# Attention in front of two mixtures of experts: another sequence for float64 weights, and two operations on other engines

## The chip, the cores and the metric

The kernel runs on one core of a Trainium2 chip. The metric is the device time of one execution, in microseconds. Five engines work in parallel, each through its own queue in the order in which the program issues its instructions: TensorE (PE in the profile, its weight loads PEld), VectorE (DVE), ScalarE (ACT), GpSimd (POOL) and SyncE (SP), which here issues all DMA transfers. An instruction starts when those ahead of it on its engine are through and when what it reads or overwrites is ready; the program inserts waits on semaphores for that.

## The reference

Three stages follow one another: causal block attention over 32 heads, a dense layer pair with `h * cos(h)`, and an eight-expert layer pair whose gates are balanced by eight rounds of row and column normalisation.

```python
scores = scale * np.matmul(q, k.transpose(0, 1, 3, 2))        # 32 heads, 576 x 64
scores = np.where(mask, scores, -1000000000.0)                # blocks of 64
scores = scores - np.max(scores, axis=-1, keepdims=True)
attn = np.exp(scores)
attn = attn / (np.sum(attn, axis=-1, keepdims=True) + 1e-09)
x = np.matmul(attn, v)                                        # to 2304 x 512
...
h = x @ w_in                                                  # w_in, w_out: float64
x = (h * np.cos(h)) @ w_out
...
for e in range(E):                                            # 8 experts
    out += P[:, e:e + 1] * (np.maximum(x @ w1[e], 0.0) @ w2[e])
```

`moe_w_in` and `moe_w_out` arrive as float64. The core has to make float32 of them itself, from the two 32-bit words of each number.

## The kernel before

All matmuls that matter run on pairs of a high and a low part of each float32 operand. The order of the work is written out by hand: each engine gets its instructions in the order in which the Python code issues them, and no scheduler moves them. What the text calls head i is one turn of the loop over the 32 heads in `attention()`.

In head i, TensorE takes the second half of the row maxima of head i + 1, the scores of head i and their product with v. Names that the text uses, with their lines:

- `px` (L265, `peak`): scores for the row maxima of the next head, in two halves u = 0 and u = 1 that share one PSUM tile. VectorE reduces each half into `nm` (L279), two reductions for u = 0 and three for u = 1. TensorE can write the second half only when the reductions of the first are done.
- `ep`, `eq`, `er`, `ec` (L303, L309, L315, L320): the exponentials on ScalarE. The start of `ep` is taken as the start of a head.
- `hi_q` (L228, L229), `hi_k` (L232), `lo` (L237 kb, L239 qb), `move` (L245, L246): the high parts of q and k for head i + 2 on ScalarE and VectorE, the low parts on GpSimd, copies between partitions by DMA.
- `turn`, `maxima` (L283, L287): the maxima of head i + 1 are transposed on TensorE and put in place by VectorE.
- `evac` (L347): ScalarE copies a head's output out of PSUM. `sums`, `fetch`, `invert` (L359), `give`, `spread` (L368): the row sums of a pair of heads are sent through DRAM, inverted on VectorE and spread over 64 partitions into `RB`.
- `scale` (L376): the division, as a product of 64 x 576 on GpSimd, into the tile `XF`. `x_hi` (L379, ScalarE) and `x_lo` (L383, GpSimd) split `XF` into the operands of the next stage.

The division runs behind the heads by pairs. In an even head i it multiplies head i - 4, in an odd head i head i - 5; at the end of the odd head follow `x_hi` and `x_lo` for both. `XF` is one buffer (a slice of a `tt` tile):

```python
RB, XF = tt[1][:, 0:S], tt[2][:, 0:S]
...
for i in range(NH):
    work = i % 6 != 5
    if i >= 4:
        scale(i - 4 - i % 2, i % 2)
    ...
    if work:
        some(2 if i else 1)
    ...
    if odd and i >= 5:
        x_hi(i - 5)
        x_lo(i - 5)
```

The conversion of the float64 weights (class `Conv`) is a generator whose steps are strewn over the heads by `some(n)`: 32 half tiles of 128 x 512, five steps each, five steps in a head, and none in every sixth head (`work`). A half tile is loaded two halves ahead (L87, 512 KB). `exponent` (L92, VectorE) takes the exponent out of the high word, `limits` (L98, L99, ScalarE) clips it and turns it into the bits of a power of two, `mantissa` (L111, L115, VectorE) builds the upper 21 and 16 further bits as a float, and `product` puts the sign onto the power (L122, VectorE) and multiplies (L124, GpSimd). The halves that are left over are converted in the first blocks of the next stage, in which GpSimd also makes the low parts of that stage's weights (L68).

Where the last heads' divisions end, the next stage's weight tiles (`jh`, L65) take over the memory that the division reads. The last two products of the pairs stand in that stage, in a table of left-over work (`leftover`).

Of the kernel before, what the change touches and what calls it, by code (L numbers as in the profile page):

```python
# [10 lines left out]
F32 = mybir.dt.float32  # L11
F32R = mybir.dt.float32r
BF16 = mybir.dt.bfloat16
I32 = mybir.dt.int32
U16 = mybir.dt.uint16
AF = mybir.ActivationFunctionType
ALU = mybir.AluOpType
# [4 lines left out]
N, DM = B * S, H * D  # L22
# [12 lines left out]
EPS = 1e-9  # L35
MASK = -1.0e30
TWO_PI = 2.0 * np.pi


@with_exitstack  # L40
def attention_moe_kernel(ctx: ExitStack, tc: tile.TileContext, qk, v, w_a, gate, w_b, out):
    nc = tc.nc
    top = ctx.enter_context(tc.tile_pool(name="top", bufs=1))
# [7 lines left out]
    nc.vector.memset(half_pi, float(np.pi / 2))  # L51
    eps = top.tile([128, 2], F32, name="eps")
    nc.vector.memset(eps, 0.0)
    e_max = top.tile([128, 1], F32, name="e_max")
    nc.vector.memset(e_max, 1171.0)
    e_all = top.tile([128, 1], F32, name="e_all")
    nc.vector.memset(e_all, 255.0 * 2.0 ** 23)


    xh = top.tile([128, NC, N], F32R, name="xh")  # L60
# [12 lines left out]
    NHALF = 2 * F1  # L73

    class Conv:
# [10 lines left out]
            src = w_a[k // 2].bitcast(I32).rearrange("p (n w) -> p n w", w=2)  # L86
            nc.sync.dma_start(out=self.w64[k], in_=src[:, (k % 2) * DM:(k % 2 + 1) * DM, :])  # L87

        def exponent(self, k):

            sc = self.sc[k] = self.scratch(1, k, [128, DM])
            nc.vector.tensor_scalar(out=sc, in0=self.w64[k][:, :, 1], scalar1=1, scalar2=21,  # L92
                                    op0=ALU.logical_shift_left, op1=ALU.logical_shift_right)

        def limits(self, k):

            sc = self.sc[k]
            nc.scalar.activation(sc, sc, AF.Relu, bias=e_max, scale=-1.0)  # L98
            nc.scalar.activation(sc, sc, AF.Relu, bias=e_all, scale=-2.0 ** 23)  # L99

        def part(self, k):
            f, o = k // 2, (k % 2) * DM
            return raw[f][:, o:o + DM]

        def mantissa(self, k):

            if k % 2 == 0:
                raw[k // 2] = wp.tile([128, 2 * DM], F32, tag="w", name="raw")
            m, w64 = self.part(k), self.w64[k]
            m21 = m.bitcast(I32)  # L110
            nc.vector.tensor_scalar(out=m21, in0=w64[:, :, 1], scalar1=0xFFFFF, scalar2=0x100000,  # L111
                                    op0=ALU.bitwise_and, op1=ALU.bitwise_or)
            yield
            mid = w64.rearrange("p n w -> p (n w)").bitcast(U16).rearrange("p (n q) -> p n q", q=4)[:, :, 1]
            nc.vector.scalar_tensor_tensor(out=m, in0=mid, scalar=2.0 ** -16, in1=m21,  # L115
                                           op0=ALU.mult, op1=ALU.add)
            yield

        def product(self, k):

            sc, m = self.sc.pop(k), self.part(k)
            nc.vector.scalar_tensor_tensor(out=sc, in0=self.w64.pop(k)[:, :, 1], scalar=-2 ** 31, in1=sc,  # L122
                                           op0=ALU.bitwise_and, op1=ALU.bitwise_or)
            nc.gpsimd.tensor_tensor(out=m, in0=m, in1=sc.bitcast(F32), op=ALU.mult)  # L124

        def run(self):

            self.load(0)
            self.load(1)
            for k in range(NHALF):  # L130
                if k:
                    self.product(k - 1)
                    if k + 1 < NHALF:
                        self.load(k + 1)
                yield
                self.exponent(k)
                yield
                self.limits(k)
                yield
                yield from self.mantissa(k)  # L140
            self.product(NHALF - 1)
            yield


# [3 lines left out]
    def attention():  # L148
        with tc.tile_pool(name="at1", bufs=1) as p1, tc.tile_pool(name="at2", bufs=2) as p2, \
# [9 lines left out]
            KA = [p1.tile([128, S], F32R, name=f"ka{j}") for j in range(2)]  # L159
# [18 lines left out]
            st, EP, EQ, ER, EC, SUMS, INV, ps_t, ps_o = ({} for _ in range(9))  # L178
# [50 lines left out]
                nc.scalar.activation(HI[64:128, :], st[i][64:128, :], AF.Copy)  # L229

            def hi_k(i):
                nc.vector.tensor_copy(out=KA[i % 2][0:64, :], in_=st[i][0:64, :])  # L232

            def lo(i):

# [137 lines left out]

            def scale(e, h):
                r = slice(64 * h, 64 * h + 64)
                nc.gpsimd.tensor_tensor(out=XF[r, :], in0=RAW[e // 2 % 2][h][r, :], in1=RB[r, :], op=ALU.mult)  # L376

            def x_hi(e):
                nc.scalar.activation(xh[:, place(e)[0], place(e)[1]], XF, AF.Copy)  # L379
# [79 lines left out]
            e = NH - 2  # L459
# [7 lines left out]
    with tc.manual_schedule():  # L467
# [174 lines left out]
        def open_group(g):  # L642

            X[g] = psh.tile([128, TB], F32, tag="h", name="hx")
            product(g, X[g], "A11", "B11", True)
            Y[g] = psh.tile([128, TB], F32, tag="h", name="hy")
            product(g, Y[g], "S1", "T1", True)


        def moe1():  # L650
            nonlocal th, tl
            with tc.tile_pool(name="m1", bufs=2) as p:
# [14 lines left out]
                def h_unit(n):  # L667
# [184 lines left out]
        for g in range(NG + 1):  # L852
            now, w = g < NG, Weights(g + 1) if g + 1 < NG else None
# [100 lines left out]
```

## Time and profile before

| | |
|---|---|
| median of 3 runs | 2243.87 us (2243.08 to 2244.49) |
| profiled execution, first to last instruction (span) | 2242.3 us |
| TensorE busy | 2158.4 us (96%) |
| VectorE busy | 1571.1 us (70%) |
| GpSimd busy | 1115.1 us (50%) |
| ScalarE busy | 1020.5 us (46%) |
| mean granted TensorE clock | 0.992 of full speed |

The profiled execution's own time is its span, 2242.3 us from its first to its last instruction; the work around it is in the runs' times alone. The busy shares are means over stages that have different limits: attention lasts from 0 to about 265 us, the dense layers to about 710, the experts take the rest. Times in the rows are us from the span's start unless marked ns. An arrow in square brackets names what ended an engine's idle time before an instruction, with that time.

### The profile page before, as it was taken

What the parts mean: (1) busy time and instruction counts of PE and PEld (TensorE: products, weight loads), DVE (VectorE), ACT (ScalarE), POOL (GpSimd) and SP (SyncE); (2) the same over time, 40 slices, a digit from 0 to 9 for tenths busy, and PEclk for the clock granted to TensorE, in tenths of its full rate; (3) what the DMA queues carried; (4) which work ended last, traced back from release to release, by engine and by line L of the source; (5) the groups of instructions that cost most, each with busy time, mean ns of one, the idle gap of its engine ahead of it and who ended that gap; (6) DMA issues with size and microseconds to landing.
All of it is one profiled execution on the core that took longest, in us unless ns stands there. A gap on an engine that the chain in (4) does not pass through costs nothing.

```text
span 2242.3 us, 29534 instructions
## 1 busy us (share of the span) xinstructions
PE 2158.4 (96%) x10869; PEld 1910.0 (85%) x10869; DVE 1571.1 (70%) x2477; ACT 1020.5 (46%) x1882; POOL 1115.1 (50%) x928
## 2 busy tenths in 40 slices
PE   7888789999998999999999999999999999999999
PEld 4555589998997888888888888888988888888988
DVE  8888776676666876666676666666676666666665
ACT  5666655555555333433344333433444434333432
POOL 5888785665554334343554434343554434344341
PEclk9999999999999999999999999999999999999999
DMA  5666410000001112121221312121221312121220
GB/s 154 167 165 175 123 34 1 1 1 1 1 19 53 61 57 75 57 76 57 76 64 50 118 61 76 57 76 58 74 69 50 118 57 76 57 76 62 71 73 31
DMA packets 74160, 152.83 MB, mean 68 GB/s; under 512 B 32896, under 2 KB 32896, under 8 KB 74016
## 3 DMA queue, kind: packets, MB, share of 16 engines
q1 hardware_dynamic: 74016, 150.95, 21.7%
q8 instruction: 85, 1.39, 0.3%
q14 instruction: 59, 0.48, 0.1%
HBM read 136.91 MB, written 4.87 MB: 63 GB/s over the span
## 4 chain that ended last, share of the span: by engine, by line
PE 64%; DVE 3%; ACT 1%; issue 0%; ACTq 0%; DVEq 0%
PE acc L474 11%; PE acc L476 11%; PE acc L475 11%; PE hx L476 6%; PE hx L474 6%; PE hx L475 6%; PE hy L474 3%; PE hy L476 3%; PE hy L475 3%; PE hz L474 1%; PE hz L475 1%; PE hz L476 1%; DVE wal L576 0%; ACT hh L810 0%; DVE hl L811 0%; DVE tl L68 0%
## 5 line engine op out<-in xcount | busy, mean ns | idle before, releaser
L585 POOL TENSOR_TENSOR wv<-stg,wv 128x512 fp32r<-128x512 f32 x190 | 335.7, 1788 | 852.7 <-ACT wv L584 852.7
L474 PE MATMUL acc<-wv,hh 128*128 128x512 f32 x1152 | 456.3, 396 | 0.0
L476 PE MATMUL acc<-wv,hl 128*128 128x512 f32 x1152 | 455.6, 395 | 0.0
L475 PE MATMUL acc<-wv,hh 128*128 128x512 f32 x1152 | 454.5, 395 | 0.0
L839 DVE SCALAR_TENSOR_TENSOR oa<-acc,P,oa 128x512 f32<-128x512 f32 x540 | 379.0, 740 | 5.2 <-PE acc L476 4.3
L810 ACT ACTIVATE hh<-c 128x384 fp32r<-128x384 f32 x288 | 151.3, 525 | 409.6 <-DVE c L896 166.0
L68 POOL TENSOR_TENSOR jl<-raw,jh 128x512 fp32r<-128x512 f32 x190 | 253.5, 1344 | 168.5 <-ACT jh L65 166.5
L811 DVE SCALAR_TENSOR_TENSOR hl<-c,hh 128x384 fp32r<-128x384 f32 x288 | 163.9, 569 | 176.4 <-ACT hh L810 176.4
L476 PEld LDWEIGHTS acc<-wv,hl 128*128 128x128 f32 x1152 | 216.0, 187 | 53.7
L475 PEld LDWEIGHTS acc<-wv,hh 128*128 128x128 f32 x1152 | 215.9, 187 | 44.0
L474 PEld LDWEIGHTS acc<-wv,hh 128*128 128x128 f32 x1152 | 216.1, 188 | 43.0
L890 DVE TENSOR_TENSOR c<-hz,c 128x384 f32<-128x384 f32 x96 | 53.4, 556 | 192.0 <-PE hz L476 192.0
L880 ACT ACTIVATE c<-hx 128x384 f32<-128x384 f32 x96 | 47.4, 494 | 282.7 <-PE hx L476 282.7
L576 DVE TENSOR_TENSOR wal<-s,wah 128x1024 fp32r<-128x1024 f32 x96 | 172.2, 1793 | 0.0
L65 ACT ACTIVATE jh<-raw 128x512 fp32r<-128x512 f32 x192 | 119.3, 622 | 99.4 <-PE acc L475 86.7
L476 PE MATMUL h<-xh,jl 128*128 128x384 f32 x384 | 132.2, 344 | 10.3 <-POOL jl L68 10.2
L687 DVE TENSOR_TENSOR hl<-g,hh 128x384 fp32r<-128x384 f32 x96 | 100.7, 1048 | 56.8 <-ACT hh L685 56.8
L474 PE MATMUL h<-xh,jh 128*128 128x384 f32 x384 | 131.6, 343 | 9.1 <-ACT jh L65 8.9
L474 PE MATMUL acc<-hh,jh 128*128 128x384 f32 x384 | 129.4, 337 | 2.2 <-DVE xl L705 1.3
L474 PE MATMUL hy<-xh,wah 128*128 128x384 f32 x384 | 129.2, 337 | 1.3 <-DVE c L896 1.3
L475 PE MATMUL h<-xl,jh 128*128 128x384 f32 x384 | 130.2, 339 | 0.0
L476 PE MATMUL hy<-xh,wal 128*128 128x384 f32 x384 | 129.1, 336 | 0.7 <-DVE wal L576 0.7
(214 smaller groups left out, 5158.4 us busy)
## 6 DMA issues: line engine op xcount, KB each, us to landing
stg<-in_w_b_dram SPq DMA_DIRECT2D x192, 512.0 KB
cw<-in_w_a_dram SPq DMA_DIRECT2D x32, 512.0 KB
st<-in_qk_dram SPq DMA_DIRECT2D x64, 144.0 KB
v<-in_v_dram SPq DMA_DIRECT2D x31, 160.0 KB
tt<-inv SPq DMA_DIRECT2D x32, 144.0 KB
out_dram<-oa SPq DMA_DIRECT2D x18, 256.0 KB
kb<-ka SPq DMA_DIRECT2D x31, 144.0 KB
qb<-qa SPq DMA_DIRECT2D x31, 144.0 KB
```

Source lines behind the costliest of these rows:

```text
L65: nc.scalar.activation(hi, src, AF.Copy)
L68: eng_lo.tensor_tensor(out=lo, in0=src, in1=hi.bitcast(F32), op=ALU.subtract)
L474: nc.tensor.matmul(ps, lh, rh, start=first, stop=False, skip_group_check=go_on)
L475: nc.tensor.matmul(ps, lh, rl, start=False, stop=False, skip_group_check=go_on)
L476: nc.tensor.matmul(ps, ll, rh, start=False, stop=last, skip_group_check=go_on)
L576: eng.tensor_tensor(out=self.al, in0=self.s, in1=self.ah.bitcast(F32), op=ALU.subtract)
L585: eng.tensor_tensor(out=t[:, DM:2 * DM], in0=src, in1=t[:, 0:DM].bitcast(F32), op=ALU.subtract)
L687: nc.vector.tensor_tensor(out=G[n][1], in0=g, in1=G[n][0].bitcast(F32), op=ALU.subtract)
L810: nc.scalar.activation(hh, src, AF.Relu)
L811: nc.vector.scalar_tensor_tensor(out=hl, in0=src, scalar=0.0, in1=hh.bitcast(F32), op0=ALU.max, op1=ALU.subtract)
L839: nc.vector.scalar_tensor_tensor(out=o, in0=acc, scalar=p, in1=o, op0=ALU.mult, op1=ALU.add)
L890: nc.vector.tensor_tensor(out=c[0], in0=z, in1=c[0], op=ALU.add)
```

## The change

The change replaces the conversion's sequence, and moves two operations.

- The conversion: `magnitude` takes the absolute value of the high word, read as float32, on ScalarE. `rounding` turns the upper 16 bits of the low word into a small integer, on ScalarE, and writes it over the low word. `clamp` and `shift` bring the magnitude into the range and place of a float32, on VectorE. `bits` puts the sign on, on VectorE, and `add` adds the small integer as int32, on GpSimd. Five steps a half tile are kept.
- `hi_k` moves from VectorE to ScalarE.
- `scale`, the division's product, moves from GpSimd to VectorE.

```diff
-        def exponent(self, k):
-            nc.vector.tensor_scalar(out=sc, in0=self.w64[k][:, :, 1], scalar1=1, scalar2=21,
-                                    op0=ALU.logical_shift_left, op1=ALU.logical_shift_right)
-        def limits(self, k):
-            nc.scalar.activation(sc, sc, AF.Relu, bias=e_max, scale=-1.0)
-            nc.scalar.activation(sc, sc, AF.Relu, bias=e_all, scale=-2.0 ** 23)
-        def mantissa(self, k):
-            nc.vector.tensor_scalar(out=m21, in0=w64[:, :, 1], scalar1=0xFFFFF, scalar2=0x100000,
-                                    op0=ALU.bitwise_and, op1=ALU.bitwise_or)
-            yield
-            nc.vector.scalar_tensor_tensor(out=m, in0=mid, scalar=2.0 ** -16, in1=m21,
-                                           op0=ALU.mult, op1=ALU.add)
-        def product(self, k):
-            nc.vector.scalar_tensor_tensor(out=sc, in0=self.w64.pop(k)[:, :, 1], scalar=-2 ** 31, in1=sc,
-                                           op0=ALU.bitwise_and, op1=ALU.bitwise_or)
-            nc.gpsimd.tensor_tensor(out=m, in0=m, in1=sc.bitcast(F32), op=ALU.mult)
+        def magnitude(self, k):
+            nc.scalar.activation(self.sc[k].bitcast(F32), self.high(k).bitcast(F32), AF.Abs)
+        def rounding(self, k):
+            nc.scalar.activation(w64[:, :, 0], mid, AF.Copy, scale=2.0 ** -13)
+        def clamp(self, k):
+            nc.vector.tensor_scalar(out=sc, in0=sc, scalar1=LEAST, scalar2=MOST, op0=ALU.max, op1=ALU.min)
+        def shift(self, k):
+            nc.vector.tensor_scalar(out=sc, in0=sc, scalar1=3, scalar2=0x3FFFFFF8,
+                                    op0=ALU.logical_shift_left, op1=ALU.bitwise_and)
+        def bits(self, k):
+            nc.vector.scalar_tensor_tensor(out=self.part(k).bitcast(I32), in0=self.high(k), scalar=-2 ** 30,
+                                           in1=self.sc.pop(k), op0=ALU.bitwise_and, op1=ALU.bitwise_or)
+        def add(self, k):
+            nc.gpsimd.tensor_tensor(out=m, in0=m, in1=self.w64.pop(k)[:, :, 0], op=ALU.add)
...
         def run(self):
...
                 if k:
-                    self.product(k - 1)
+                    self.add(k - 1)
                     if k + 1 < NHALF:
                         self.load(k + 1)
                 yield
-                self.exponent(k)
+                self.magnitude(k)
                 yield
-                self.limits(k)
+                self.rounding(k)
+                self.clamp(k)
                 yield
-                yield from self.mantissa(k)
-            self.product(NHALF - 1)
+                self.shift(k)
+                yield
+                self.bits(k)
+                yield
+            self.add(NHALF - 1)
...
             def hi_k(i):
-                nc.vector.tensor_copy(out=KA[i % 2][0:64, :], in_=st[i][0:64, :])
+                nc.scalar.activation(KA[i % 2][0:64, :], st[i][0:64, :], AF.Copy)
...
             def scale(e, h):
-                nc.gpsimd.tensor_tensor(out=XF[r, :], in0=RAW[e // 2 % 2][h][r, :], in1=RB[r, :], op=ALU.mult)
+                nc.vector.tensor_tensor(out=XF[r, :], in0=RAW[e // 2 % 2][h][r, :], in1=RB[r, :], op=ALU.mult)
```

The diff is cut to its core: lines that only name views of the same tiles and two constants that fall away are left out. In the changed kernel the lines of `attention()` stand four further down.

How the queues read before and after is shown at three places. In these rows "waits" lists the semaphores that an instruction waits for, by the engine that raises them (Pool is GpSimd, DMAHW are transfers). Where nothing is listed, the order of the queue or an earlier wait covers it.

VectorE, from the end of an odd head to the next even head (heads 7 and 8), before:

```order
L287 TENSOR_TENSOR qa_100<-pt,diag 5x640 [waits PE_49]
L111 TENSOR_SCALAR raw<-cw 128x512
L115 SCALAR_TENSOR_TENSOR raw<-cw,raw 128x512 [waits DVE_49]
L279 TENSOR_REDUCE nm_110<-px 128x1 [waits PE_49]
L279 TENSOR_REDUCE nm_110<-px 128x1
L122 SCALAR_TENSOR_TENSOR tla<-cw,tla 128x512 [waits Activation_49]
L92 TENSOR_SCALAR tla<-cw 128x512 [waits DMAHW5_49,Pool_49]
```

VectorE at the same place in the changed kernel (L291 is L287 of before, L107 clamp, L111 shift, L118 bits, L380 the division's product into `XF`, a `tt` tile, L283 the reductions):

```order
L107 TENSOR_SCALAR tla<-tla 128x512 [waits Activation_49]
L291 TENSOR_TENSOR qa_96<-pt,diag 5x640 [waits PE_49]
L111 TENSOR_SCALAR tla<-tla 128x512 [waits DVE_49]
L118 SCALAR_TENSOR_TENSOR raw<-cw,tla 128x512 [waits DMAHW4_49,DVE_49]
L380 TENSOR_TENSOR tt<-tla,tt 64x576 [waits DMAHW6_49,Pool_49]
L283 TENSOR_REDUCE nm_106<-px 128x1 [waits PE_49]
```

The conversion's steps between the reductions are gone, and the product with a wait for GpSimd stands ahead of them.

GpSimd, from an odd head into the next even head, before (L124 the conversion's product, L237 kb, L239 qb, L383 x_lo, L376 the division's product):

```order
L376 TENSOR_TENSOR tt<-tt 64x576 [waits DMAHW5_49]
L124 TENSOR_TENSOR raw<-raw,tla 128x512 [waits DVE_49,Pool_49]
L237 TENSOR_TENSOR kb_107<-st,ka_103 64x576 [waits DMAHW6_49,DVE_49,PE_49]
L239 TENSOR_TENSOR qb_105<-st,hi 64x576 [waits DMAHW7_49,Activation_49,Pool_49]
L383 TENSOR_TENSOR xl<-tt,xh 128x576 [waits Activation_49,Pool_49]
L376 TENSOR_TENSOR tt<-tla,tt 64x576 [waits DMAHW6_49,Pool_49]
L124 TENSOR_TENSOR raw<-raw,tla 128x512 [waits DVE_49]
```

GpSimd at the same place in the changed kernel (L124 is now the add, L241 kb, L243 qb, L387 x_lo):

```order
L124 TENSOR_TENSOR raw<-raw,cw 128x512 [waits DVE_49,DMAHW3_49,Activation_49,Pool_49]
L241 TENSOR_TENSOR kb_103<-st,ka_99 64x576 [waits DMAHW6_49,PE_49,Activation_49]
L243 TENSOR_TENSOR qb_101<-st,hi 64x576 [waits DMAHW7_49,Pool_49]
L387 TENSOR_TENSOR xl<-tt,xh 128x576 [waits Activation_49,Pool_49]
L124 TENSOR_TENSOR raw<-raw,cw 128x512 [waits DMAHW4_49,DVE_49]
```

Both products of the division are gone from the queue. kb now waits for ScalarE (Activation), where k's high part is made, and x_lo is followed by the add.

ScalarE in an odd head of the changed kernel, from the last exponential on (L96 magnitude, L232 and L233 q's high part, L236 k's, L102 rounding, L383 x_hi):

```order
L324 ACTIVATE ec<-sc 64x64 [waits PE_49,Activation_49]
L96 ACTIVATE tla<-cw 128x512 [waits DMAHW4_49]
L232 ACTIVATE qa_97<-st 64x576 [waits DMAHW7_49,DMAHW1_49]
L233 ACTIVATE hi<-st 64x576 [waits Activation_49,Pool_49]
L236 ACTIVATE ka_99<-st 64x576 [waits DMAHW6_49,DMAHW0_49]
L102 ACTIVATE cw<-cw 128x512
L383 ACTIVATE xh<-tt 128x576 [waits DVE_49]
```

Before, two passes of `limits` stood behind q's high part; now one pass of the conversion stands ahead of it, and k's high part is between.

## Rows read from the trace of the kernel before

**Rows 1.** Busy time by stretch: us, engines' busy us, clock, DMA share, GB/s

```profile
150.00:200.00 50.00, 40.84 (x193) 27.84 (x191) 44.08 (x69) 34.74 (x61) 41.80 (x28) 0.97 0.60 163
...
400.00:500.00 100.00, 98.82 (x566) 96.72 (x565) 70.28 (x108) 54.87 (x101) 60.87 (x46) 1.00 0.00 1
```

**Rows 2.** First exponential of each head, whole run, then 60 to 255 us

```profile
L303 ACT ACTIVATE ep<-sp x32: 583/599/604, 17.1 to 259.9; 128x512 f32<-128x512 f32 x32
...
L303 ACT ACTIVATE ep<-sp x25: 597/599/602, 62.0 to 253.3; 128x512 f32<-128x512 f32 x25
```

**Rows 3.** Who waited for whom, TensorE, 60 to 255 us: total, times, longest

```profile
PE px L265 <- DVE nm L279: 24.9, 20, 1.7
```

**Rows 4.** Conversion on VectorE, 60 to 255 us: ns minimum/median/maximum

```profile
L122 DVE SCALAR_TENSOR_TENSOR tla<-cw,tla x21: 679/682/1075, 62.8 to 254.1; 128x512 int32<-128x512 int32 x21
...
L92 DVE TENSOR_SCALAR tla<-cw x20: 416/420/1723, 63.7 to 239.8; 128x512 int32<-128x512 int32 x20
...
L111 DVE TENSOR_SCALAR raw<-cw x20: 426/685/939, 67.8 to 243.8; 128x512 int32<-128x512 int32 x20
...
L115 DVE SCALAR_TENSOR_TENSOR raw<-cw,raw x20: 1795/1802/1811, 68.7 to 244.8; 128x512 f32<-128x512 uint16 x20
```

**Rows 5.** Timeline of head 18: start, us, engine, line; GpSimd and VectorE together

```profile
159.05 1.72 POOL L376 TENSOR_TENSOR tt<-tla,tt 64x576 f32<-64x576 f32 x1
...
159.44 1.71 DVE L92 TENSOR_SCALAR tla<-cw 128x512 int32<-128x512 int32 x1
```

**Rows 6.** Timeline of head 17, ScalarE

```profile
148.29 0.74 ACT L347 ACTIVATE tla<-o,eps 65x576 f32<-65x576 f32 x1 [0.96 <-PE o L341]
...
149.46 0.60 ACT L303 ACTIVATE ep<-sp 128x512 f32<-128x512 f32 x1 [0.43 <-PE sp L296]
...
151.38 0.68 ACT L228 ACTIVATE qa<-st 64x576 fp32r<-64x576 f32 x1
```

**Rows 7.** Timeline of head 17, hand-over from VectorE to GpSimd

```profile
154.00 0.44 DVE L232 CAST ka<-st 64x576 fp32r<-64x576 f32 x1
...
154.58 1.40 POOL L237 TENSOR_TENSOR kb<-st,ka 64x576 fp32r<-64x576 f32 x1 [2.40 <-issue]
...
157.54 1.43 POOL L383 TENSOR_TENSOR xl<-tt,xh 128x576 fp32r<-128x576 f32 x1
```

**Rows 8.** Prices of single forms: groups (count, busy us, mean ns), timeline of head 15

```profile
L68 DVE TENSOR_TENSOR jl<-raw,jh 128x512 fp32r<-128x512 f32 x2 | 1.3, 690 | 5.8 <-ACT jh L65 5.8
...
136.99 1.32 POOL L124 TENSOR_TENSOR raw<-raw,tla 128x512 f32<-128x512 f32 x1 [0.96 <-DVE tla L122]
...
L98 ACT ACTIVATE tla<-tla,e_max 128x512 int32<-128x512 int32 x20 | 14.4, 722 | 6.6 <-DVE tla L92 6.4
```

**Rows 9.** A weight load of head 14 (timeline, SP), and a later stretch

```profile
129.38 0.34 SPq L87 DMA_DIRECT2D cw<-in_w_a_dram  x1
...
135.00:135.50 0.50, 0.13 (x2) 0.00 (x0) 0.50 (x1) 0.50 (x2) 0.50 (x1) 1.00 0.00 0
```

**Rows 10.** Timeline of head 14, VectorE and ScalarE: reductions to the next head

```profile
127.46 1.29 DVE L279 TENSOR_REDUCE nm<-px 128x1 f32<-128x448 f32 x2
...
133.73 0.60 ACT L303 ACTIVATE ep<-sp 128x512 f32<-128x512 f32 x1 [0.41 <-PE sp L296]
```

**Rows 11.** Busy time by stretch in head 13 (columns as in rows 1)

```profile
118.50:120.00 1.50, 0.00 (x0) 0.00 (x0) 1.47 (x4) 1.45 (x4) 1.18 (x1) 1.00 0.08 9
...
120.50:124.00 3.50, 3.50 (x8) 1.72 (x7) 1.77 (x5) 2.02 (x3) 2.84 (x3) 0.51 0.85 251
```

**Rows 12.** Timeline behind the attention stage: waits in square brackets

```profile
267.19 1.39 POOL L376 TENSOR_TENSOR tt<-raw,tt 64x576 f32<-64x576 f32 x1
...
268.62 1.67 ACT L65 ACTIVATE jh<-raw 128x512 fp32r<-128x512 f32 x3 [3.46 <-POOL tt L376]
...
303.44 0.68 ACT L379 ACTIVATE xh<-tt 128x576 fp32r<-128x576 f32 x1 [4.78 <-POOL tt L376]
...
305.20 0.69 PE L474 MATMUL h<-xh,jh 128*128 128x384 f32 x1 [2.87 <-ACT jh L65]
```

More of the change, by code (lines that the diff above doesn't have):

```diff
@@ L37 @@
 TWO_PI = 2.0 * np.pi
+LEAST, MOST = (float(np.array([b], np.uint32).view(np.float32)[0]) for b in (0x38100000, 0x47EFFFFF))
 @with_exitstack
@@ L53, in attention_moe_kernel @@
     nc.vector.memset(eps, 0.0)
[L54 to L57, printed above, removed]
     xh = top.tile([128, NC, N], F32R, name="xh")
@@ L87, in load, with high @@
             nc.sync.dma_start(out=self.w64[k], in_=src[:, (k % 2) * DM:(k % 2 + 1) * DM, :])
-        def exponent(self, k):
-            sc = self.sc[k] = self.scratch(1, k, [128, DM])
-            nc.vector.tensor_scalar(out=sc, in0=self.w64[k][:, :, 1], scalar1=1, scalar2=21,
-                                    op0=ALU.logical_shift_left, op1=ALU.logical_shift_right)
-        def limits(self, k):
-            sc = self.sc[k]
-            nc.scalar.activation(sc, sc, AF.Relu, bias=e_max, scale=-1.0)
-            nc.scalar.activation(sc, sc, AF.Relu, bias=e_all, scale=-2.0 ** 23)
+        def high(self, k):
+            return self.w64[k][:, :, 1]
         def part(self, k):
@@ L103, in part @@
             return raw[f][:, o:o + DM]
-        def mantissa(self, k):
+        def magnitude(self, k):
+            self.sc[k] = self.scratch(1, k, [128, DM])
+            nc.scalar.activation(self.sc[k].bitcast(F32), self.high(k).bitcast(F32), AF.Abs)
+        def rounding(self, k):
+            w64 = self.w64[k]
+            mid = w64.rearrange("p n w -> p (n w)").bitcast(U16).rearrange("p (n q) -> p n q", q=4)[:, :, 1]
+            nc.scalar.activation(w64[:, :, 0], mid, AF.Copy, scale=2.0 ** -13)
+        def clamp(self, k):
+            sc = self.sc[k].bitcast(F32)
+            nc.vector.tensor_scalar(out=sc, in0=sc, scalar1=LEAST, scalar2=MOST, op0=ALU.max, op1=ALU.min)
+        def shift(self, k):
+            sc = self.sc[k]
+            nc.vector.tensor_scalar(out=sc, in0=sc, scalar1=3, scalar2=0x3FFFFFF8,
+                                    op0=ALU.logical_shift_left, op1=ALU.bitwise_and)
+        def bits(self, k):
             if k % 2 == 0:
                 raw[k // 2] = wp.tile([128, 2 * DM], F32, tag="w", name="raw")
-            m, w64 = self.part(k), self.w64[k]
-            m21 = m.bitcast(I32)
-            nc.vector.tensor_scalar(out=m21, in0=w64[:, :, 1], scalar1=0xFFFFF, scalar2=0x100000,
-                                    op0=ALU.bitwise_and, op1=ALU.bitwise_or)
-            yield
-            mid = w64.rearrange("p n w -> p (n w)").bitcast(U16).rearrange("p (n q) -> p n q", q=4)[:, :, 1]
-            nc.vector.scalar_tensor_tensor(out=m, in0=mid, scalar=2.0 ** -16, in1=m21,
-                                           op0=ALU.mult, op1=ALU.add)
-            yield
-        def product(self, k):
-            sc, m = self.sc.pop(k), self.part(k)
-            nc.vector.scalar_tensor_tensor(out=sc, in0=self.w64.pop(k)[:, :, 1], scalar=-2 ** 31, in1=sc,
-                                           op0=ALU.bitwise_and, op1=ALU.bitwise_or)
-            nc.gpsimd.tensor_tensor(out=m, in0=m, in1=sc.bitcast(F32), op=ALU.mult)
+            nc.vector.scalar_tensor_tensor(out=self.part(k).bitcast(I32), in0=self.high(k), scalar=-2 ** 30,
+                                           in1=self.sc.pop(k), op0=ALU.bitwise_and, op1=ALU.bitwise_or)
+        def add(self, k):
+            m = self.part(k).bitcast(I32)
+            nc.gpsimd.tensor_tensor(out=m, in0=m, in1=self.w64.pop(k)[:, :, 0], op=ALU.add)
         def run(self):
```

## Prediction

> **What bounds the kernel now.** I began with the busy table by stage. In the MoE stages TensorE is busy 98.8 of 100 us, in attention 40.8 of 50, where VectorE has 44.1 and GpSimd 41.8 [rows 1]. The MoE stages are the multiplier's own; whatever the change does, it does in attention and just behind it. So next I read the length of a head, from one start of `ep` (the first exponential, L303) to the next: heads 0 to 31 start at 17.1 to 259.9 us, heads 6 to 30 at 62.0 to 253.3 [rows 2]. That is 191.3 / 24 = 7.97 us a head, **47.8 us for six heads** (the pattern repeats after six, since every sixth head carries no weight conversion), and (62.0 - 17.1) / 6 = 7.48 us in the first six heads, which have no division yet. The waits then say who holds TensorE: the second half of the score maxima (`px`) waits for VectorE's reductions of the first half (`nm`), 24.9 us in 20 waits, 1.25 us each [rows 3]. VectorE is late because the conversion stands ahead of those reductions in its queue: the sum L115 takes 1.80 us every time, the others 0.42 to 1.72 [rows 4].
>
> Why so long: L92 began 0.39 us into a GpSimd multiply of 1.72 us and took 1.71 us, where its fastest is 0.42 [rows 4, 5]. It ended 0.38 us behind that multiply. So a VectorE operation of this kind stands still until GpSimd's running one ends, and the saved work must be priced with that.
>
> **Part by part.** VectorE loses, for each half tile, L92, L111 and L115, and once a head the high part of k (0.44 us [rows 7]). It gains clamp and shift, priced as L92 and L111, their nearest forms: 0.42 us each if nothing blocks, up to 1.72 if GpSimd does [rows 4]. The `bits` operation is of L122's form, 0.68 to 1.08 [rows 4]. The division's product comes to VectorE: 0.69 us for 512 columns [rows 8], so 0.78 for 576 (estimate by columns). By the medians VectorE is relieved of 0.42 + 0.69 + 1.80 + 0.44 - 0.42 - 0.42 - 0.78 = 1.7 us in a head with conversion. ScalarE swaps two passes of 0.72 for two of the same size (bounds 0.60, an exponential of that width, to 0.72 [rows 6, 8]) and gains k's high part, 0.68 by its sister L228 [rows 6]. GpSimd loses the product and swaps a float product for an integer add, taken at 1.32 as that product ran unhindered [rows 8]. No row shows an integer add there. Half or twice that are the bounds: it counts once in six heads below, so 0.66 x 4.33 = 2.9 us less or 1.32 x 4.33 = 5.7 more.
>
> On SP no transfer moves, but the load of the next half tile now waits for GpSimd's add where it waited for VectorE's sign step, and q, k and the copies stand behind it. In the chain below the add of an even head ends about 11.6 us after the odd head's `ep`; the half is first read at 17.5 + 1.9 = 19.4. A load issued at 129.38 had landed by 135.0, when no DMA engine moved anything [rows 9]: 5.6 us at most against 7.8 of room, so nothing. If that room went, ScalarE would stand at `magnitude` with q's and k's high parts behind it.
>
> **The new wait** is what I base the number on. `XF` is one buffer. GpSimd's x_lo reads it late in every odd head, and the product of the next even head overwrites it. Both were GpSimd's, in order. Now the product is VectorE's, it must wait for x_lo, and both reductions of `px` queue behind it. Followed from `ep` of an odd head:
> - four exponentials until the q copy starts: 151.38 - 149.46 = 1.92 [rows 6];
> - magnitude 0.72, two q copies and k's, 3 x 0.68: 2.76, so 4.68;
> - hand-over to GpSimd 154.58 - 154.44 = 0.14, then kb, qb and x_lo, 157.54 + 1.43 - 154.58 = 4.39 [rows 7]: 9.21;
> - hand-over 0.14, product 0.78, reductions 1.29 [rows 10]: 11.42;
> - from there TensorE's own queue to the next `ep`: 133.73 - 128.75 = 4.98 in an even head [rows 10]: **16.40 us for two heads**.
>
> Where the odd head has no conversion, the magnitude falls out: 15.68. Six heads take at least 2 x 16.40 + 15.68 = 48.5 us, 0.7 more than now, although VectorE has less to do.
>
> To this come the waits of VectorE and GpSimd for one another. In a head with conversion, shift and bits (0.42 + 0.68) are queued ahead of the product while kb, qb and x_lo run, and get in between them: 17.50. Without conversion the add of the half before is ready when x_lo ends and goes first, 1.32: 17.00. Six heads: 52.0, **4.2 more than now**. If the add goes ahead of the product in the other pairs too, 18.82 and 54.6: 6.8 more. Bounds 0.7 and 6.8; I take 4.2, as the rows of L92 and L115 show such waits as the rule. Heads 6 to 31 are 4.33 times six: +18.2 (3.0 to 29.5).
>
> The Trainium skill (page SBUF — State Buffer, section Who interferes with whom) says that a VectorE operation with two SBUF inputs, or in a two-port mode, and a GpSimd operation reading SBUF exclude each other for whole instructions: "the other fully blocks". It speaks against this change, since the product on VectorE still contends with GpSimd. The trace agrees (1.71 us for 0.42 of work). With that rule the sum is 52.0 for six heads, without it 48.5.
>
> **The clock.** After 1.5 us without a matmul TensorE's granted clock fell to 0.51, the 1.2 GHz level, for 3.5 us in which TensorE was busy throughout [rows 11]: 1.7 us lost. The mean of 0.97 over 50 us [rows 1] is one such fall in about six heads. The wait in the even heads grows by 17.5 - 15.9 = 1.6 to some 2.8 us, so I expect a fall in each of the three even heads of six, two more than now, at half that price, because part of the slow time is spent waiting: 2 x 0.85 x 4.33 = +7.4. Bounds: the four present falls vanish, -7.4; all fall at full price, (3 x 1.7 - 1.7) x 4.33 = +14.7.
>
> **Gains.** In the first six heads ScalarE needs 0.74 for the output copy, 0.43 of waiting for scores, 1.92 + 2.76 and the rounding's 0.72: 6.57 [rows 6, 8]. They can come down from 7.48 to that (-5.5) or stay (0); I take half, -2.8. Behind attention ScalarE idles 3.46 us for two GpSimd products, which at 0.78 instead of 1.39 release it 1.2 sooner [rows 12]. A little later it idles 4.78 for two more, and TensorE 2.87 behind it [rows 12]; I take 1.6 back there. Together -2.8 (0 to -7). VectorE's relief in the first MoE blocks I cost at nothing: TensorE waits for ScalarE and GpSimd there.
>
> **Sum.** 18.2 + 7.4 - 2.8 - 2.8 = +20.0 us on the profiled span of 2242.3, so 2262.3. The median of the runs lies 1.6 above the span: **2264 us**.
>
> **Rivals.**
> 1. Faster by a hidden wait. The price is that of the waits between VectorE and GpSimd, and it decides whether the product finds its place right behind x_lo. If shift and bits fall where GpSimd idles anyway and the idle stretches come out too short for falls of the clock: 3.0 - 7.4 - 2.8 - 2.8 = -10, 2234 us. For it: GpSimd has one operation less a head. Against it: L115 never took under 1.79 us in this stage. It decides once a pair of heads costs under 15.9. Chance 0.10.
> 2. The chain through x_lo is not the last. Then VectorE's relief counts in full and ScalarE bounds the heads, 6.57 and in every second head x's high part, about another pass of 0.72: 6.9. (6.9 - 7.97) x 26 = -28, with the first heads and the end -33: 2211. It would need x_lo to end some 3 us sooner than ScalarE's and GpSimd's rows allow. Chance 0.04.
> 3. The worse order. The add goes first in every pair, and the clock falls in each even head at full price: 29.5 + 14.7 - 2.8 - 2.8 = +38.6, 2282. For it: the add waits for nothing of VectorE's that is late. Chance 0.17. A slow integer add would end up here too.
> 4. Losses and gains cancel, within 0.2%: chance 0.07. That is 4.5 us, about what a measurement of this kernel can tell from no change.
>
> The forecast has the remaining 0.62.
>
> **How the numbers follow.** Slower by over 0.2%: forecast and rival 3, 0.79. Faster: rivals 1 and 2, 0.14. Same: 0.07. The range goes up over rival 3 to 2287 and down to 2244, no change at all; below lie rivals 1 and 2, above it little more than 0.05.
>
> **What the profile after would show.** Right: the product on VectorE waits for x_lo (GpSimd) 13 times, 1 to 4 us each; TensorE's wait for `nm` doubles and more; long even heads and shorter odd ones, pairs near 17.5; the last head starts 20 to 26 us later than 259.9; more clock falls. Single steps: clamp and shift mostly over 0.42, integer add about 1.3 to 1.5. Wrong: even heads under 8 us, or the product ready as soon as its queue reaches it.

## The result, and the profile after

The changed kernel takes **2278.29 us** (median of 5 runs, 2263.44 to 2289.37) where the kernel before takes 2244.46 in the same series: ratio 1.0147, interval 1.0122 to 1.0172, so slower. The profiled execution is the one of 2263.44 us, the shortest of the five (the first profile below). Its span is 2261.6 us; the forecast's sum gave 2262.3 for the span and 2264 for the median.

The first exponentials of the heads in this profile, whole run:

```profile
L307 ACT ACTIVATE ep<-sp x32: 597/599/603, 18.0 to 280.4; 128x512 f32<-128x512 f32 x32
```

The last head starts at 280.4 us, 20.5 later than in [rows 2]. Heads 6 and 30 start at 67.8 and 274.9, which is 51.8 us for six heads (before 47.8). The stretch of [rows 1], columns as there:

```profile
150.00:200.00 50.00, 41.20 (x179) 27.93 (x179) 36.55 (x56) 33.41 (x59) 27.68 (x19) 0.90 0.58 149
```

VectorE and GpSimd have 7.5 and 14.1 us less to do than in [rows 1]. TensorE is as busy as before, at a granted clock of 0.90 instead of 0.97. Relief was given, and TensorE got through fewer matmuls (179 for 193). Who waited for whom from 60 to 255 us, TensorE, then VectorE:

```profile
PE px L269 <- DVE nm L283: 34.2, 16, 3.0
...
DVE qa L291 <- PE pt L287: 29.8, 23, 3.0
DVE nm L283 <- PE px L269: 22.1, 24, 1.2
```

TensorE's wait for `nm` is 2.1 us each instead of 1.25 [rows 3]. But the wait on which the forecast rests, the product's for x_lo on GpSimd, is in no row of VectorE. And the long heads are the odd ones: from head 6 on the even heads take 6.3 us in the mean and the odd ones 11.0. The place shows in the timeline of the end of head 10 and of head 11 (start 108.58), VectorE:

```profile
107.03 1.34 DVE L111 TENSOR_SCALAR tla<-tla 128x512 int32<-128x512 int32 x1
108.41 1.81 DVE L118 SCALAR_TENSOR_TENSOR raw<-cw,tla 128x512 int32<-128x512 int32 x1
110.14 0.24 DVE L363 RECIPROCAL sc<-sc 72x16 f32<-72x16 f32 x1
110.41 0.76 DVE L380 TENSOR_TENSOR tt<-tt 64x576 f32<-64x576 f32 x1
111.20 1.29 DVE L283 TENSOR_REDUCE nm<-px 128x1 f32<-128x448 f32 x2
...
117.75 1.14 DVE L380 TENSOR_TENSOR tt<-tla,tt 64x576 f32<-64x576 f32 x1
```

GpSimd and TensorE in the same head:

```profile
106.68 1.41 POOL L241 TENSOR_TENSOR kb<-st,ka 64x576 fp32r<-64x576 f32 x1 [3.31 <-ACT ka L236]
108.17 1.50 POOL L243 TENSOR_TENSOR qb<-st,hi 64x576 fp32r<-64x576 f32 x1
...
115.63 1.40 POOL L387 TENSOR_TENSOR xl<-tt,xh 128x576 fp32r<-128x576 f32 x1
...
112.64 1.03 PE L269 MATMUL px<-ka,qa 68*128 68x256 f32 x3 [2.71 <-DVE nm L283]
```

The shift (0.43 alone) stands until kb is through, and the bits (0.69 alone) until qb is; such waits of VectorE for GpSimd's running instruction are called waits at the port below. The product comes on top of these two, and the reductions of `px` start behind all three. TensorE stands still for 2.71 us, and its granted clock falls (columns as in rows 1):

```profile
113.10:116.60 3.50, 3.50 (x10) 1.98 (x9) 0.89 (x3) 0.07 (x1) 3.35 (x3) 0.58 0.83 227
```

TensorE is busy throughout, mostly at the 1.2 GHz level ("half clock" below). The odd head becomes 10.8 us long by it, and so x_lo, through at 117.03, is done when VectorE comes to the next product at 117.75. One wait hides the other. The trace has a stretch at half clock in every odd head from 3 to 29; before it was one odd head in three.

The prices of single forms, from 60 to 255 us: minimum, median, maximum in ns

```profile
L111 DVE TENSOR_SCALAR tla<-tla x18: 426/540/1607, 72.2 to 245.4; 128x512 int32<-128x512 int32 x18
L118 DVE SCALAR_TENSOR_TENSOR raw<-cw,tla x18: 693/1794/1968, 72.7 to 247.0; 128x512 int32<-128x512 int32 x18
L124 POOL TENSOR_TENSOR raw<-raw,cw x19: 1279/1751/1866, 65.3 to 249.0; 128x512 int32<-128x512 int32 x19
L96 ACT ACTIVATE tla<-cw x19: 644/652/661, 69.6 to 248.7; 128x512 f32<-128x512 f32 x19
```

The integer add takes 1.28 us alone, ScalarE's new passes 0.65. The bits stand at 1.79 in the median, where the forecast had 0.68 to 1.08: they took over the place of L115, and with it L115's wait [rows 4].

### The profile page after: what moved, and what is told of

The parts are those of the page before. It is cut to its first block, busy times and chain, and to the rows that moved or that the text cites. A ratio compares the mean times of both kernels' runs of the same rounds, so it can differ in the third digit from the quotient of the medians.

```text
span 2261.6 us, 29615 instructions
## 1 busy us (share of the span) xinstructions
PE 2173.5 (96%) x10869; PEld 1918.9 (85%) x10869; DVE 1553.2 (69%) x2444; ACT 1030.6 (46%) x1913; POOL 1063.2 (47%) x896
## 4 chain that ended last, share of the span: by engine, by line
PE 64%; DVE 3%; ACT 0%; issue 0%; ACTq 0%; DVEq 0%
PE acc L478 11%; PE acc L479 11%; PE acc L480 11%; PE hx L478 6%; PE hx L480 6%; PE hx L479 6%; PE hy L480 3%; PE hy L478 3%; PE hy L479 3%; PE hz L478 1%; PE hz L480 1%; PE hz L479 1%; DVE wal L580 0%; DVE hl L815 0%; ACT hh L814 0%; DVE oa L837 0%
## 5 line engine op out<-in xcount | busy, mean ns | idle before, releaser
L478 PE MATMUL hx<-th,wah 128*128 128x384 f32 x384 | 129.0, 336 | 1.0 <-ACT c L884 1.0
```

Source lines behind the costliest of these rows:

```text
L478: nc.tensor.matmul(ps, lh, rh, start=first, stop=False, skip_group_check=go_on)
```

## The experiments

**The changed kernel again** (run last, shown first). The runs of one kernel lie 26 us apart, and the first profile is of the shortest. So it was run once more, unaltered.

> The changed kernel once more, unaltered, for a profile of an execution nearer to its median of 2278 us than the profiled one of 2263 us. If its executions differ by the number of even heads in which the product waits for x_lo (the forecast's wait, which the profiled execution shows nowhere), a profile of 2272 us or more shows that wait at least 3 times between 60 and 255 us, with 2.5 us or more of TensorE's wait for nm behind each, and the more of them the longer the run. If the slower executions differ by anything else, the wait for x_lo stays absent and the extra time stands elsewhere (a later start, a longer second stage). A profile of 2268 us or less tells neither.

Measured: 2286.63 us (6 runs, 2264.27 to 2297.27), ratio 1.0166 (1.0132 to 1.0199). The profiled execution is that of 2297.27, span 2295.5 (the second profile below). Heads; then TensorE's and VectorE's waits from 60 to 255 us:

```profile
L307 ACT ACTIVATE ep<-sp x32: 596/599/601, 18.1 to 315.2; 128x512 f32<-128x512 f32 x32
...
PE px L269 <- DVE nm L283: 46.1, 17, 5.3
...
DVE tt L380 <- POOL xl L387: 23.3, 10, 3.7
```

Here the forecast's wait is there, in each of the ten even heads of the stretch, 1.30 to 3.71 us each (from head 6 to head 30 thirteen times, 31.1 us). Now the even heads are the long ones (13.2 us, the odd ones 6.7). Timeline behind head 11, which starts at 116.85; VectorE and GpSimd:

```profile
121.13 0.83 DVE L291 TENSOR_TENSOR qa<-pt,diag 5x640 fp32r<-5x640 f32 x1 [1.06 <-PE pt L287]
125.35 1.82 DVE L380 TENSOR_TENSOR tt<-tla,tt 64x576 f32<-64x576 f32 x1 [3.39 <-POOL xl L387]
...
123.90 1.42 POOL L387 TENSOR_TENSOR xl<-tt,xh 128x576 fp32r<-128x576 f32 x1
125.28 1.28 POOL L124 TENSOR_TENSOR raw<-raw,cw 128x512 int32<-128x512 int32 x1
...
128.64 1.03 PE L269 MATMUL px<-ka,qa 68*128 68x256 f32 x3 [3.66 <-DVE nm L283]
```

x_lo ends 8.47 us behind the start of head 11; in the first profile it was 117.03 - 108.58 = 8.45. The chain is the same in both. What differs is when VectorE asks: after 5.1 us here, after 9.2 there. And where the wait is, GpSimd's integer add starts first and the product stands 1.82 us instead of 0.74: the order of rival 3. Six heads take 59.7 us, and at half clock the core spent 88.7 us before 330 us (first profile 61.4, before 27.3). The other spans and clocks of this series go together (2262.5 us at 0.986, 2291.3 at 0.980). That executions in between are mixtures of the two patterns fits that, but no profile of one was taken; nor did any run show what sends an execution into one or the other.

**Extra matmuls, in the kernel after and before.** Fourteen more matmuls per odd head, whose products nobody reads, to keep TensorE from standing still at the place of the clock fall.

```diff
+                    if i % 2:
+                        for _ in range(14):
+                            nc.tensor.matmul(ps[0:64, 256:512], KB[i % 2][:, 512:576], QB[i % 2][:, 320:576],
+                                             start=True, stop=True)
```

> The changed kernel with 14 more matmuls of 256 columns (about 1.7 us) in each odd head, between the last scores and the second half of px; they write columns that nobody reads. Clock theory: in the changed kernel the odd heads' idle time of some 2.7 us costs little by itself, the fall of the granted clock behind it costs 1.7 us a pair. The filler leaves under 1.3 us idle, the falls go from about 20 to under 6, a pair of heads from 17.1 to about 15.4, the time by some 20 us to about 2258. If the falls are a by-product and the wait itself is the loss (or the wait for XF, which this does not touch), the time stays at 2278 or rises by what of the filler does not fit the idle time (up to 10 us).

> The kernel before with the same filler in its odd heads. Clock theory: its four falls (1.7 us each, heads 7, 13, 19, 25) vanish, -7 us, and in the odd heads whose idle time is under 1.7 us the filler adds up to 0.4 us each, +4: 2240 to 2244. If the clock does not matter: +4 to +8.

Measured: after 2306.64 us, ratio 1.028 (1.0266 to 1.0294), above both theories; before 2244.75, ratio 1.0003 (0.9994 to 1.0012). In the changed kernel the odd heads did become short (7.8 us), but the falls were not taken away: they moved to the even heads (12.7 us), behind the wait for x_lo, and the time at half clock before 330 us was 68.3 us (first profile 61.4). TensorE's and VectorE's waits, 60 to 255 us:

```profile
PE px L269 <- DVE nm L283: 41.9, 9, 5.0
...
DVE tt L384 <- POOL xl L391: 22.7, 10, 3.7
```

So with the falls out of the odd heads the forecast's wait is there, as in the second profile. How much of the added time is the extra matmuls' own was not separated: they take some 1.6 us in an odd head, and a pair of heads takes 20.5 us where it takes 19.9 in the second profile. Before, the time at half clock fell from 27.3 to 13.7 us and nothing was gained: the odd heads went from 8.6 to 8.2 us, the even ones from 7.4 to 7.7.

**The product back on GpSimd.**

```diff
-                nc.vector.tensor_tensor(out=XF[r, :], in0=RAW[e // 2 % 2][h][r, :], in1=RB[r, :], op=ALU.mult)
+                nc.gpsimd.tensor_tensor(out=XF[r, :], in0=RAW[e // 2 % 2][h][r, :], in1=RB[r, :], op=ALU.mult)
```

> The changed kernel with the division's product back on GpSimd. Port theory (shift, bits and product stand ahead of px's reductions in VectorE's queue and each lets one GpSimd operation pass first): the product's 0.75 to 1.8 us leave the queue ahead of the reductions, TensorE's idle time in odd heads falls to 1.2 to 1.9 us, some falls of the clock go: 2245 to 2265. XF theory (the forecast's): the wait of VectorE for x_lo is gone altogether, even heads shorten, 2240 or less, and the odd heads keep their length.

Measured: 2248.82 us, ratio 1.0022 (1.0013 to 1.0032), in the port theory's range and above that of the XF theory. Six heads 48.0 us, half clock 37.5 us. TensorE still waits for `nm`, but 1.5 us each instead of 2.1 (60 to 255 us):

```profile
PE px L269 <- DVE nm L283: 31.7, 21, 3.3
```

The other two parts of the change, together, cost 5 us and gain nothing; some 30 come with the product.

**The conversion's steps earlier.** Clamp, shift and bits right behind the first reductions, where GpSimd idles; the product stays at the head's end.

```diff
                 if work:
-                    some(1)
+                    some(3 if i else 1)
                 if odd and i >= 5:
...
-                if work:
+                if work and not i:
                     some(2)
```

> The changed kernel with shift and bits moved, in emission order, to right behind clamp, between the second reductions and the maxima, where GpSimd idles. Port theory: both run at 0.43 and 0.69, nothing but the product stands ahead of the reductions, TensorE's idle time in odd heads is under 1.3 us, the falls go: pairs of 13.5 to 14.5 us, 2225 to 2240, faster than the kernel before. XF theory: unchanged waits in even heads, 2270 to 2280.

Measured: 2288.96 us, ratio 1.02 (1.0186 to 1.0214): a miss for the theory of the port, and above the XF theory's 2270 to 2280. Shift and bits indeed never waited, and the product did (rows of the two forms, then VectorE's waits, 60 to 255 us):

```profile
L118 DVE SCALAR_TENSOR_TENSOR raw<-cw,tla x17: 691/693/694, 72.7 to 254.3; 128x512 int32<-128x512 int32 x17
...
L380 DVE TENSOR_TENSOR tt<-tla,tt x10: 1817/1818/1820, 66.3 to 240.9; 64x576 f32<-64x576 f32 x10
...
DVE tt L380 <- POOL xl L387: 39.0, 10, 4.0
```

Even heads 13.1, odd ones 6.2: the pattern of the second profile. Only this run has a profile; the four runs lie close together (2286.97 to 2289.61). So the waits at the port are one way into the loss, and without them the forecast's wait takes over in full.

**The product later, two attempts.** In both the product moves behind the second reductions; the first also has the conversion's steps early. By the move each product of an odd head i (it takes the second head of the pair, head i - 4) follows the broadcast of the next reciprocals, so it divides by the sums of the next pair, and waits for that transfer.

```diff
-                if i >= 4:
-                    scale(i - 4 - i % 2, i % 2)
                 if i:
                     evac(i - 1)
...
+                if i >= 4:
+                    scale(i - 4 - i % 2, i % 2)
                 if odd and i >= 5:
                     x_hi(i - 5)
```

> The changed kernel with two moves in VectorE's order and nothing else: the clamp, the shift and the bits stand right behind the first reductions of a head (as in the run before), and the division's product stands behind the second reductions, next to the conversion of x, instead of ahead of them. Theory (TensorE waits for VectorE because the product, which must wait for x_lo on GpSimd, stands ahead of the reductions that TensorE waits for): no wait of TensorE for nm above 2.5 us, no clock fall between 60 and 255 us, heads of about 7.0 us, the last head starts near 240 us, span some 30 us below the kernel before: 2210 to 2225 us. Rival (the product's place is indifferent; what costs is the extra work on VectorE in sum): the last head still starts at 275 us or later and the time is 2270 to 2290 us. A second rival (x_hi and x_lo, now later, hold up something behind them): the time is 2235 to 2260 us with a new wait for x_hi or x_lo.

> The changed kernel with the product alone behind the second reductions; clamp, shift and bits stay where the change has them. If the wait behind x_lo is the whole cost: as the run with both moves, within 5 us of it. If the waits of the shift and the bits while GpSimd holds the port (1.3 to 1.8 us at the end of a head) cost a clock fall by themselves: odd heads of 9 to 10 us stay, the last head starts at 255 us or later, 2240 to 2265 us.

Measured: 2265.21 us, ratio 1.0093 (1.0076 to 1.011), and 2287.3, ratio 1.0192 (1.0177 to 1.0207). Neither tells the theories apart. The wait for x_lo is gone from VectorE's rows, and another is in its place (first of the two):

```profile
DVE tt L380 <- DMA tt<-inv: 35.7, 11, 6.4
```

**Parts alone.** The old conversion with the product on VectorE and k's high part on ScalarE; the changed kernel with k's high part on VectorE; the kernel before with the product on VectorE as the only edit.

```diff
             def hi_k(i):
-                nc.scalar.activation(KA[i % 2][0:64, :], st[i][0:64, :], AF.Copy)
+                nc.vector.tensor_copy(out=KA[i % 2][0:64, :], in_=st[i][0:64, :])
```

> The kernel before with two parts of the change: the product on VectorE and k's high part on ScalarE; the conversion is the old one. If the product's place behind x_lo is the cause whatever the conversion is, pairs of heads take 17 to 19 us and the time is 2260 to 2285 us. If it needs the new conversion's longer GpSimd add and its two clamp and shift waits, 2235 to 2250 us.

> The changed kernel with k's high part back on VectorE. The load on ScalarE falls by one 0.68 us copy per head and that of VectorE rises by about as much. If ScalarE's chain (magnitude, rounding, k's high part) makes kb and qb late on GpSimd and so x_lo, the time falls to 2245 to 2260 us; if VectorE's own load at the end of a head is what TensorE waits for, it rises to 2285 to 2300 us; no difference: 2263 to 2289 us.

> The kernel before with the product on VectorE as the only edit. If the product's 0.75 us at the end of each head, ahead of the reductions that TensorE waits for, is what costs (TensorE's wait grows to 1.8 us or more and its clock falls in every odd head), the odd heads take 10 to 11 us, the last head starts 15 to 40 us later than before and the time is 2255 to 2285 us. If it needs the high part of k on ScalarE or the new conversion beside it, the time is 2240 to 2250 us.

| product | conversion | k's high part | us | ratio |
|---|---|---|---|---|
| GpSimd | old | VectorE | 2244 | 1 |
| GpSimd | new | ScalarE | 2248.82 | 1.0022 (1.0013 to 1.0032) |
| VectorE | old | VectorE | 2270.39 | 1.0118 (1.0104 to 1.0132) |
| VectorE | old | ScalarE | 2262.55 | 1.0085 (1.0064 to 1.0106) |
| VectorE | new | VectorE | 2285.46 | 1.0187 (1.0172 to 1.0202) |
| VectorE | new | ScalarE | 2278.29, 2286.63 | 1.0147, 1.0166 |

The product alone costs 26 us, and with the old conversion too both waits stand in the rows (the product alone; TensorE and VectorE, 60 to 255 us):

```profile
PE px L265 <- DVE nm L279: 34.6, 19, 3.1
...
DVE tt L376 <- POOL xl L383: 16.4, 8, 3.1
```

For the product alone the time, the wait for `nm` (1.8 us each) and the last head's later start (28.7 us) are as its expectation has them; the odd heads of 10 to 11 us are not: the even heads take 9.6, the odd ones 8.2. With k's high part on ScalarE as well, the time of 2262.55 is in the range for the product's place behind x_lo, but in that profile VectorE waits for x_lo only 3 times, 2.2 us in all, and the odd heads are the long ones (10.1 us). Beside the product on VectorE the new conversion costs 15 us more (2285.46 against 2270.39). k's high part on ScalarE is a gain there with the old conversion, 8 us (2262.55 against 2270.39); with the new one the runs do not tell it (2285.46 against 2278.29 and 2286.63). That it would free x_lo's chain on ScalarE if it went back was a miss. Neither was run alone with the product on GpSimd.

**The product later, with the broadcast behind it.** The edit of the two attempts, and `spread(i - 3)` moved behind the product, so that each product reads its own pair's reciprocals. With the conversion's steps early, and without.

```diff
-                if odd and i >= 3:
-                    spread(i - 3)
                 if i + 3 < NH:
...
                 if i >= 4:
                     scale(i - 4 - i % 2, i % 2)
+                if odd and i >= 3:
+                    spread(i - 3)
                 if odd and i >= 5:
```

> The changed kernel with the product behind the second reductions of a head, the broadcast of the reciprocals behind it (so that each product reads its own pair's reciprocals), and clamp, shift and bits behind the first reductions. Nothing is left on VectorE between the copy of qa and the reductions that TensorE waits for. If that place is the cause, the wait of TensorE for nm stays under 1.5 us, there is no clock fall in the odd heads, and the time is 2205 to 2235 us. If VectorE's work ahead of the copy of qa (2.6 us more than before) becomes the next wait of the scores, heads of 7.5 to 8.5 us and 2240 to 2265 us.

> As the run with both moved, but the shift and the bits stay at the head's end where the change has them; the product alone goes behind the second reductions, with the broadcast of the reciprocals behind it. If the product was what made the wait of TensorE too long, the heads come back to those of the kernel before and the time is 2225 to 2250 us. If the bits' wait for the port (1.3 to 1.8 us) is enough by itself for a clock fall, odd heads of 9 to 11 us remain and the time is 2255 to 2280 us.

Measured: with both moves **2233.82 us**, ratio 0.9958 (0.9945 to 0.997); with the product's alone 2236.68, ratio 0.9965 (0.9952 to 0.9979). Both beat the kernel before and the changed one. With both moves, heads, and waits from 60 to 255 us:

```profile
L307 ACT ACTIVATE ep<-sp x32: 597/598/602, 18.0 to 249.1; 128x512 f32<-128x512 f32 x32
...
PE sp L300 <- DVE qa L291: 18.3, 15, 2.4
PE px L269 <- DVE nm L283: 1.1, 2, 0.8
...
DVE nm L283 <- PE px L269: 33.9, 30, 2.3
```

TensorE's wait for `nm` went from 34.2 us to 1.1, and VectorE's for x_lo is gone. Six heads take 45.5 us. What is left stands where the second theory put it, at the copy of qa, which now follows clamp, shift, bits and product; the time lies just under the first theory's upper bound. That theory's other sign, no clock fall in the odd heads, did not come in full: the time at half clock is 34.1 us (before 27.3), and of its five stretches between 60 and 255 us two begin in odd heads, so the gain over the kernel before is not one of the clock. With the product's move alone the bits still wait:

```profile
L118 DVE SCALAR_TENSOR_TENSOR raw<-cw,tla x20: 691/1797/1812, 71.7 to 243.0; 128x512 int32<-128x512 int32 x20
...
PE px L269 <- DVE nm L283: 28.0, 20, 2.5
```

and the clock falls as rarely as in the kernel before (27.3 us at half clock); six heads take 46.6 us. So the bits at the port are not enough for a fall in every odd head; with the product behind them it came in every odd head of the first profile. The same conversion and the same engines as in the changed kernel gain 10 us on the kernel before once these steps stand elsewhere in VectorE's queue: the place costs, not the work.

## Why the prediction was right, and where it was not

The direction and its cause (the product on VectorE, ahead of the reductions that TensorE waits for) held, and the time is in the range: 2264 was forecast, 20 us more than before, and 2278.29 came, 34 more. The prediction's own signs of being wrong, even heads under 8 us and a product that is ready when its queue reaches it, both stand in the first profile (6.3 us, and no wait for x_lo); of its signs of being right the wait for x_lo, the doubled wait for `nm` (2.7 us each) and the long even heads stand in the second, where pairs take 19.9 us instead of 17.5 and the last head starts 55 us later than before instead of 20 to 26. Of its steps:

- **The chain to x_lo was right almost to the digit.** Worked out for an odd head without conversion it is 9.21 - 0.72 = 8.49 us from `ep` to x_lo's end; the two profiles show 8.45 and 8.47 in head 11. With conversion it is 9.21, and the rows of x_lo give 9.06 to 9.22 in the first profile and 9.42 to 9.62 in the second.
- **The wait for x_lo was real but conditional.** "The product on VectorE waits for x_lo (GpSimd) 13 times, 1 to 4 us each" holds in the second profile (thirteen times from head 6 to head 30, ten of them between 60 and 255 us), and not once in the first. The step that failed is "in a head with conversion, shift and bits (0.42 + 0.68) are queued ahead of the product while kb, qb and x_lo run, and get in between them". They do, but for 1.34 + 1.81 instead of 1.10, in the even heads, and with the product that holds TensorE for 2.7 us by itself. A rival of that kind (the end of the even head, not x_lo, holds the reductions) was missing. The second profile and the earlier conversion show that the two waits stand in for one another.
- **"Long even heads and shorter odd ones, pairs near 17.5"**: the first profile has the odd ones long, pairs of 51.8 / 3 = 17.3; the second the even ones, pairs of 59.7 / 3 = 19.9. Of the single steps, the clamp was not held up (0.42 in the median), and the add was more than forecast, 1.75 in the median.
- **The clock was mis-sized.** "At half that price, because part of the slow time is spent waiting" fails: in the first profile TensorE was busy in 3.50 of 3.50 us of the slow stretch, so the full 1.7 us fell due. The way from the reductions to the next `ep`, 4.98 in [rows 10], was 119.39 - (111.20 + 1.29) = 6.90 there, 1.92 more. In the second profile it was 8.01 from `px` alone (128.64 to the start of head 13 at 136.65); its stretches at half clock are longer (15 stretches, 88.7 us; the first profile 16, 61.4).
- **The first six heads**: forecast -2.8, measured +4.9 (49.8 against 44.9 us). Head 3 already falls, before any product is made: shift 1.47 and bits 1.80 stand ahead of the reductions, timeline of VectorE and TensorE from the end of head 2 into head 3:

```profile
38.65 1.47 DVE L111 TENSOR_SCALAR tla<-tla 128x512 int32<-128x512 int32 x1
40.15 1.80 DVE L118 SCALAR_TENSOR_TENSOR raw<-cw,tla 128x512 int32<-128x512 int32 x1
...
43.59 0.62 PE L269 MATMUL px<-ka,qa 68*128 68x256 f32 x3 [2.06 <-DVE nm L283]
```

  The mis-sized term is the bits' price: L115's place, not L122's form, sets it. With these steps and the product elsewhere (both moves, at the end of the experiments) the first six heads took 42.0 us, 2.9 less than before; with the conversion's steps alone moved they took 46.5, so the bits are not all of it.
- **The end**: forecast -2.8, measured -1.1 from the last head's start to the end (1981.25 us against 1982.35), in the second profile -2.1. The two products on VectorE released ScalarE only 0.4 us sooner (its wait there is 3.02 us, 3.46 in [rows 12]) where 1.2 was forecast, and TensorE still waits 4.48 us for ScalarE's `jh`.
- **The sum**, 2262.3, meets the first profile's 2261.6 partly by chance: the first head starts 0.9 later, six heads take 4.9 more where -2.8 stood, the next 24 take 15.8 more and the last one 1.1 less where 25.6 stood for heads 6 to 31, and the end 1.1 less: +19.4. In the second profile the same parts are +1.0, +2.0, +47.5, +4.7 and -2.1, +53.2 together. So the term of heads 6 to 31, 18.2 + 7.4, measured 14.7 in one execution and 52.3 in the other, and the median lies between them.
- **Rival 3** (2282) is what the second profile does, the add ahead of the product and falls at full price and more (span 2295.5). Its 0.17 was too low: of the eleven runs of the changed kernel seven lie above 2278. **Rival 1** rested on the waits at the port; without them (the conversion's steps early) it came out at 2289, not 2234. **Rival 2**'s condition, that x_lo's chain is not the last, was met in the first profile, and the time still rose, because the waits at the port and the falls took its place; it was met again when the product and the broadcast moved, which gained 10 us, not 33.
- **The rule on the shared port** (the Trainium skill, SBUF — State Buffer, section Who interferes with whom): the bits have two SBUF inputs and took 1.81 us where they overlap qb, ending 0.55 behind it, and never over 0.69 where they were moved away from GpSimd's work. The trace agrees with "the other fully blocks", but for 0.14 us: alone the bits take 0.69.

## What to carry to other kernels

Moving an operation to an engine with free time moves it into that engine's order: look at what stands behind it there, and whether the operation can wait for anything. If it can, put it behind what others wait for; against the product on GpSimd (2248.82 us) the same product on VectorE costs some 30 us in one place of the queue (2278.29) and gains 12 in another (2236.68). And when two waits can hide one another, take both away before judging either: with the odd heads' clock falls alone driven out (2306.64 us), or the waits at the port alone taken away (2288.96), this kernel was no faster.

## What was not expected

One program settled into two patterns: executions of the changed kernel take 2263 to 2297 us, those of the kernel before 2243.1 to 2245.4. The runs of the early conversion lie within 2.6 us, and the one with a profile shows the second pattern. What chooses between them was not found.

A stretch at half clock also has a feedback: in the first profile it lengthened the odd heads so far that the wait for x_lo vanished. Driving the falls out of the odd heads by more matmuls made the changed kernel 28 us slower (2306.64 against 2278.29), and the kernel before no faster.

A second `XF`, which would remove the wait for x_lo alone, was not tried.
